# Retention and a gated feed-forward layer on one core: exponential decay tables, both first loads split over two queues, and the last 128 output rows in three parts

## The chip, the cores and the metric

The kernel runs on one core of a Trainium2 chip. The metric is the device time of one execution in microseconds (us); the time of a kernel is the median of its runs. The names of the engines are those of the profile: PE is TensorE (matmuls), PEld its weight loads, DVE is VectorE, ACT is ScalarE, POOL is GpSimd, SP is SyncE. A q behind the name (SPq, ACTq) is the engine's sequencer, which issues DMAs.

## The reference

Inputs are q, k and v of shape (8, 8, 576, 64) (batch B, heads H, sequence S, head dimension D) and three weights of a feed-forward layer, w_gate and w_val (512 x 1536) and w_out (1536 x 512), all in float32. The first stage is a retention without softmax, the second a layer with a sigmoid gate:

```
scale = 1 / sqrt(D);  gamma[h] = 1 - 2 ** (-5 - h)
scores = scale * (q @ k^T)                         # per batch and head
Dmat[h, i, j] = gamma[h] ** (i - j) if i >= j else 0
attn = (scores * Dmat) @ v                         # (B, H, S, D)
x = attn.transpose(0, 2, 1, 3).reshape(B * S, H * D)   # 4608 x 512
out = (sigmoid(x @ w_gate) * (x @ w_val)) @ w_out      # 4608 x 512, float32
```

Since gamma ** (i - j) is gamma ** i times gamma ** -j, the decay can be put on q and k ahead of the product: q is multiplied by scale * gamma ** i and k by gamma ** -j.

## The kernel before

**Stages.** The order of all instructions is written out by hand (a manual schedule); each engine and each queue runs its own in that order. The first 768 output columns of x (transposed, `xT`) come from three "pairs" of 256 tokens (`PAIRS`), the rest from steps of 128 tokens (`STEPS`), whose work is put between the matmuls of the feed-forward blocks (`BLOCKS`, of 256 to 512 tokens). PE's work from about 17 us to the end is thus a continuous row of feed-forward matmuls (`h_units`, `op_units`) with the retention's small products in between.

**First loads.** `load_pair` brings the pairs in tiles of 256 KB (`k32p`, `q32p`, `v32p`: 128 partitions, four heads, two rows of 64 numbers per partition, 512 bytes in a row). For the first two pairs the order on SP is k and q of heads 0 to 3, k and q of heads 4 to 7 of pair 0, the same of pair 1, then the four v tiles, then the weights. SP issues them one after the other; only the very first k tile goes out in two halves, from SP and from ScalarE (L130). The tiles of all loads come from a pool of 18 buffers, so a later load waits for the cast that frees its buffer.

**Decay tables.** Two pairs of small tables hold gamma ** -j for k and scale * gamma ** i for q: `ktab2`, `qtab2` for the pairs (positions step by 2 over partitions), `ktab`, `qtab` for the steps. The class `Tables` makes them: GpSimd writes the positions (`iota`), VectorE multiplies them by ln gamma for each of the eight heads (`args`, L207), ScalarE takes two sigmoids, of the argument and of its negative (`sigmoids`, L210 and L211), and VectorE makes the powers out of their quotients (`powers`, L214 to L216: one reciprocal and two products). The second tables' work is interleaved: four args, the first tables' powers, four args, the sigmoids; their powers come after the first q cast (L876). ScalarE's only tables in the kernel are thus those of the sigmoid, which the gate needs too. `lnscale` and `warm`, which the change adds, are not there.

**First products.** `cast_pair` (L288) multiplies a loaded tile by its table and writes bf16, k on GpSimd and q on VectorE; v is cast on GpSimd (L285). `turn` (`pair_t`) transposes a cast tile on PE against the identity (L328) and copies the result out on ScalarE (L338). `pair_qk` (L347) makes the scores, which VectorE masks (L352); `first_st` (L383) the state products; `tile_sv` (L401) copies the state into a block-diagonal tile `sbd`, four of which are set to zero ahead of use (two at L238, two at L878). `fill` (L188) runs matmuls on a zero tile whose results nobody reads. The order on PE is: kT, qT of heads 0 to 3, a fill, the scores, kT, a fill, qT of heads 4 to 7, a fill, and so on with pair 1.

**The end.** `op_units` multiplies the gated tokens `gvs` (12 chunks of 128) by `wo_sb`. For every 128 rows there are 12 matmuls of 512 columns into a bank of PSUM (L809), a copy on ScalarE and a store by SP (`store`, `leave`, L780). The last 128 rows (L793 to L806) go in two halves of 256 columns: 12 matmuls (L798), a copy on VectorE and a store from SP for the first half; 12 matmuls, a copy on ScalarE and a store from ScalarE's queue for the second. Three banks (`ffn_psum`) take the results of all of these in turn.

Of the kernel before, what the change touches and what calls it, by code (L numbers as in the profile page):

```python
# [9 lines left out]
FP32 = mybir.dt.float32  # L10
BF16 = mybir.dt.bfloat16
AF = mybir.ActivationFunctionType
ALU = mybir.AluOpType
# [3 lines left out]
def kernel(  # L17
# [19 lines left out]
    nc = tc.nc  # L37

    B, H, S, D = q.shape
    NT, DM = out.shape  # L40
    DFF = moe_w_gate.shape[1]
    P = 128
    M = H // 2
    NC = (S + P - 1) // P
# [3 lines left out]
    consts = ctx.enter_context(tc.tile_pool(name="consts", bufs=1))  # L48
# [5 lines left out]
    osb_pool = ctx.enter_context(tc.tile_pool(name="osb", bufs=13))  # L54
# [6 lines left out]
    ffn_psum = ctx.enter_context(tc.tile_pool(name="ffn_psum", bufs=3, space=PS))  # L61
# [5 lines left out]
    LAST = NC - 1  # L67
# [23 lines left out]
    def rows(col, n):  # L91

        out_ = []
        for c0 in sorted(rows_of):
            for r0, w in rows_of[c0]:
                lo, hi = max(c0, col), min(c0 + w, col + n)
                if lo < hi:
                    x = (lo - col, r0 + lo - c0, hi - lo)
                    if out_ and out_[-1][1] + out_[-1][2] == x[1]:
                        out_[-1] = (out_[-1][0], out_[-1][1], out_[-1][2] + x[2])  # L100
                    else:
                        out_.append(x)
        return out_


    def half(x):
        return slice(x * 64, x * 64 + 64)
# [17 lines left out]
    def load_pair(A):  # L125

        b, a2 = PAIRS[A]
        for nm, src, g in (("k", k, 0), ("q", q, 0), ("k", k, 1), ("q", q, 1), ("v", v, 0), ("v", v, 1)):
            t = ld_pool.tile([P, M, 2, D], FP32, tag="ld", name=f"{nm}32p_{A}_{g}")
            queues = (nc.sync, nc.scalar) if A == 0 and g == 0 and nm == "k" else (nc.sync,)  # L130
            n = M // len(queues)
            for i, queue in enumerate(queues):
                queue.dma_start(  # L133
                    out=t[:, i * n:(i + 1) * n].rearrange("p h r d -> p h (r d)"),
                    in_=src[b, g * M + i * n:g * M + (i + 1) * n,
                            a2 * 2 * P:(a2 + 1) * 2 * P, :].rearrange("h (p r) d -> p h (r d)", r=2))
            parts[nm, "pair", A, g] = t
            yield
# [11 lines left out]
    def load_wo(f):  # L150
        t = ld_pool.tile([P, DM], FP32, tag="ld", name=f"wo32_{f}")
        nc.sync.dma_start(out=t, in_=moe_w_out[f * P:(f + 1) * P, :])
        parts["o", f] = t

    both = [load_pair(A) for A in range(2)]
    for n_pair in (4, 2):
        for one in both:
# [5 lines left out]
    load_w(4, 4)  # L163
    load_w(8, 4)
    pair_2 = load_pair(2)
    for n_wo, n_pair in ((2, 4), (6, 2), (4, 0)):
        for _ in range(n_wo):
# [16 lines left out]
    def fill(n, parts=1):  # L184

        for i in range(n * parts):
            k = 4 // parts
            nc.tensor.matmul(idle[-1][:, 0:k, :], lhsT=blank, rhs=blank.unsqueeze(1).to_broadcast([P, k, P]),  # L188
                             start=True, stop=True)

    fill(10, 4)
    class Tables:


        def __init__(self, shape, pattern, step, put):
            def tile_of(name, dims):
                return consts.tile(dims, FP32, name=f"{name}{step}")
            self.put = put
            self.pos = tile_of("pos", [P, pattern[0][1], pattern[1][1]])
            nc.gpsimd.iota(self.pos, pattern=pattern, base=0, channel_multiplier=step,  # L200
                           allow_small_or_imprecise_dtypes=True)
            self.arg, self.q, self.k = (tile_of(name, shape) for name in ("arg", "qtab", "ktab"))
            self.both, self.inv = (tile_of(name, [P, 2] + shape[1:]) for name in ("both", "inv"))

        def args(self, heads):
            for h in heads:
                nc.vector.tensor_scalar_mul(self.put(self.arg, h), self.pos, math.log(1.0 - 2.0 ** (-5.0 - h)))  # L207

        def sigmoids(self):
            nc.scalar.activation(out=self.both[:, 0], in_=self.arg, func=AF.Sigmoid)  # L210
            nc.scalar.activation(out=self.both[:, 1], in_=self.arg, func=AF.Sigmoid, scale=-1.0)  # L211

        def powers(self):
            nc.vector.reciprocal(out=self.inv, in_=self.both)  # L214
            nc.vector.tensor_tensor(out=self.k, in0=self.both[:, 1], in1=self.inv[:, 0], op=ALU.mult)
            nc.vector.scalar_tensor_tensor(out=self.q, in0=self.both[:, 0], scalar=1.0 / math.sqrt(D),  # L216
                                           in1=self.inv[:, 1], op0=ALU.mult, op1=ALU.mult)

    tabs2 = Tables([P, 2, H, 2], [[2 * P, 2], [1, 2]], 2, lambda t, h: t[:, :, h, :])
    tabs2.args(range(H))  # L220
    tabs2.sigmoids()
    qtab2, ktab2 = tabs2.q, tabs2.k
    ident = consts.tile([P, P], BF16)
    make_identity(nc, ident)


    tabs1 = Tables([P, NC, H, 1], [[P, NC], [1, 1]], 1, lambda t, h: t[:, :, h, :])
    nc.vector.tensor_scalar_add(tabs1.pos[half(1), LAST], tabs1.pos[half(1), LAST], -64.0)
    tabs1.args(range(M))
    tabs2.powers()  # L230
    tabs1.args(range(M, H))
    tabs1.sigmoids()
    qtab, ktab = (t.rearrange("p c h o -> p c (h o)") for t in (tabs1.q, tabs1.k))


    sbd = [consts.tile([P, M, P], BF16, name=f"sbd{i}") for i in range(4)]
    for t in sbd[:2]:
        nc.vector.memset(t, 0.0)  # L238

    trip = consts.tile([P, 2, P], BF16)  # L240
# [1 line left out]
    for p0 in (0, 64):  # L242
        nc.gpsimd.affine_select(out=trip[p0:p0 + 64], in_=trip[p0:p0 + 64], compare_op=ALU.is_ge, fill=0.0,
                                base=0, pattern=[[-1, 2], [1, P]], channel_multiplier=-2)
# [12 lines left out]
    wo_sb = consts.tile([P, NFC, DM], BF16)  # L257
# [6 lines left out]
    on_pool, on_act, on_dve = nc.gpsimd.tensor_copy, nc.scalar.copy, nc.vector.tensor_copy  # L264
# [10 lines left out]
    def cast_pair(nm, A, g, eng):  # L275

        if (nm, A) not in natural:
            natural[nm, A] = osb_pool.tile([P, 2, H, D], BF16, tag="osb", name=f"{nm}p_{A}")
        if nm != "v" and A == 2:
            o = natural[nm, A].rearrange("p r (m y) d -> p y m r d", y=2)[:, g]  # L280
        else:
            o = natural[nm, A][:, :, g * M:(g + 1) * M, :].rearrange("p r h d -> p h r d")
        i = parts.pop((nm, "pair", A, g))
        if nm == "v":
            eng(out=o, in_=i)  # L285
        else:
            tab = (ktab2 if nm == "k" else qtab2)[:, PAIRS[A][1], g * M:(g + 1) * M, :].unsqueeze(3).to_broadcast([P, M, 2, D])
            eng.tensor_tensor(out=o, in0=i, in1=tab, op=ALU.mult)  # L288
# [493 lines left out]
    def store(opp, r0, eng=None):  # L782

        ob = osb_pool.tile([P, DM], FP32, tag="osb", name=f"ob_{r0}")
        (eng or on_act)(out=ob, in_=opp)  # L785
        stores.append((r0, ob))
        if len(stores) > KEEP:
            leave()

    def op_units(gvs, t0, n):  # L790
        for nb in range(n // P):
            r0 = t0 + nb * P
            if r0 == NT - P:  # L793

                for i, queue in enumerate((nc.sync, nc.scalar)):
                    opp = ffn_psum.tile([P, 256], FP32, tag="ffn", name=f"op_{t0}_{nb}_{i}")
                    for fc in range(NFC):
                        nc.tensor.matmul(opp, lhsT=gvs[fc][:, nb * P:(nb + 1) * P],  # L798
                                         rhs=wo_sb[:, fc, i * 256:(i + 1) * 256],
                                         start=(fc == 0), stop=(fc == NFC - 1))  # L800
                    ob = osb_pool.tile([P, 256], FP32, tag="osb", name=f"ob_{r0}_{i}")
                    (nc.vector.tensor_copy if i == 0 else nc.scalar.copy)(out=ob, in_=opp)
                    for p0, at_row, w in rows(r0, P):
                        queue.dma_start(out[at_row:at_row + w, i * 256:(i + 1) * 256], ob[p0:p0 + w])
                    yield 6 * 512
                return  # L806
            opp = ffn_psum.tile([P, 512], FP32, tag="ffn", name=f"op_{t0}_{nb}")
            for fc in range(NFC):
                nc.tensor.matmul(opp, lhsT=gvs[fc][:, nb * P:(nb + 1) * P], rhs=wo_sb[:, fc, :],  # L809
                                 start=(fc == 0), stop=(fc == NFC - 1))  # L810
                if fc % 4 == 3 and fc < NFC - 1:
                    yield 4 * 512
            store(opp, t0 + nb * P)
            yield 4 * 512
# [14 lines left out]
    gvs = {}  # L829
# [43 lines left out]
    turn("k", 0, 0, *TR)  # L873
    turn("q", 0, 0, *PV)
    fill(3)
    tabs1.powers()  # L876
    for t in sbd[2:]:
        nc.vector.memset(t, 0.0)  # L878
    cast_pair("q", 0, 1, nc.vector)
    pair_qk(0, 0, QK)  # L880
    turn("k", 0, 1, *TR)
# [233 lines left out]
```

## Time and profile before

| what | value |
|---|---|
| median of 3 runs (lowest to highest) | 331.42 us (330.25 to 331.87) |
| the profiled execution: time, span | 331.87 us, 330.2 us |
| mean granted TensorE clock | 1.000 |
| PE busy | 320.9 us, 97% of the span |
| PEld, DVE, ACT, POOL busy | 169.5, 149.9, 139.3, 104.8 us |
| read from HBM, written | 37.75 MB, 9.44 MB |
| narrow matmuls of the last rows (L798) | 24, 273 ns each from start to end, 0.11 us from one start to the next |
| ACT table loads (L210) | 1, 1283 ns |
| args for 4 and for 5 positions per head (L207) | 8 of 207 ns and 8 of 316 ns in the mean |
| powers: reciprocals (L214), products (L215, L216) | 553 and 634 ns; 193 and 761, 184 and 186 ns |

The span runs from the first to the last instruction of the profiled execution; its whole time is 1.7 us longer. Matmuls are pipelined, so the busy time of one (273 ns) is more than what it adds to a row of them. Slices, groups, chain and timeline of one execution belong together; another run of the same kernel differs by up to 1.6 us here.

### The profile page before, as it was taken

The page shows a single profiled execution, that of the slowest core. Times are in us where ns is not written, and L with a number is a line of the kernel's source. Part 1 is how long each engine was busy: PE and PEld are TensorE (multiplying, and loading weights), DVE is VectorE, ACT ScalarE, POOL GpSimd, SP SyncE. Part 2 cuts the span into 40 slices and gives each one's busy share as a digit, 9 for nine tenths or more (in the row PEclk, how much of TensorE's full clock was granted, in tenths as well). Part 3 has the DMA queues.
Part 4 walks back from the last instruction along what each step waited for, and adds up shares of the span by engine and source line. Part 5 has one row for each costly group of instructions (what it writes and reads, how often), then busy time and mean ns, then how long its engine had stood idle before and what let it go on. Part 6 is the DMA issues. An engine that isn't in the chain of part 4 may idle for free.

```text
span 330.2 us, 8760 instructions
## 1 busy us (share of the span) xinstructions
PE 320.9 (97%) x3618; PEld 169.5 (51%) x3618; DVE 149.9 (45%) x340; ACT 139.3 (42%) x315; POOL 104.8 (32%) x138
## 2 busy tenths in 40 slices
PE   7899999998999999999999999999999999999996
PEld 5564557845645654445444544455445544544443
DVE  8845637655624454345343543434435444404310
ACT  4664555554424344325433453335334533343321
POOL 5585545534545563108400750065003000000000
PEclk9999999999999999999999999999999999999999
DMA  7999999999999999948992699259904910010003
GB/s 205 293 358 379 336 280 214 187 144 192 183 196 190 214 199 226 215 92 154 221 222 45 131 238 229 45 108 230 208 0 92 333 59 0 33 68 34 2 32 95
DMA packets 145833, 55.14 MB, mean 167 GB/s; under 512 B 125184, under 2 KB 137728, under 8 KB 145792
## 3 DMA queue, kind: packets, MB, share of 16 engines
q1 hardware_dynamic: 145376, 54.31, 76.5%
q8 instruction: 28, 0.46, 0.6%
q10 hardware_dynamic: 416, 0.26, 0.2%
q14 instruction: 13, 0.11, 0.1%
HBM read 37.75 MB, written 9.44 MB: 143 GB/s over the span
## 4 chain that ended last, share of the span: by engine, by line
PE 91%; DMA 4%; SPq 2%; DVE 1%; ACT 1%; issue 0%; POOL 0%; ACTq 0%
PE h L742 50%; PE op L809 23%; PE op L994 3%; PE hg L846 3%; PE hv L846 3%; DMA T<-qk 2%; SPq L133 2%; PE val L553 2%; DMA v32p<-in_v_dram 2%; PE row L527 1%; PE val L569 1%; PE row L535 1%; PE op L798 1%; PE hg L920 1%; PE hv L920 1%; PE st L383 0%
## 5 line engine op out<-in xcount | busy, mean ns | idle before, releaser
L770 DVE TENSOR_TENSOR gv<-g,h 128x512 bf16<-128x512 bf16 (+1 forms) x96 | 62.9, 655 | 103.5 <-PE h L742 99.3
L742 PE MATMUL h<-xT,wv_sb 128*128 128x512 bf16 (+2 forms) x432 | 100.7, 355 | 0.0
L742 PE MATMUL h<-xT,wg_sb 128*128 128x512 bf16 (+2 forms) x432 | 100.7, 355 | 0.0
L766 ACT ACTIVATE g<-h 128x512 bf16<-128x512 f32 (+1 forms) x96 | 54.8, 571 | 95.5 <-PE h L742 91.3
L809 PE MATMUL op<-wo_sb,gv 128*128 128x512 bf16 x372 | 84.0, 379 | 0.0
L742 PEld LDWEIGHTS <-wg_sb 128*128 128x128 bf16 x432 | 42.0, 98 | 41.1
L742 PEld LDWEIGHTS <-wv_sb 128*128 128x128 bf16 x432 | 42.0, 98 | 40.3
L809 PEld LDWEIGHTS <-gv 128*128 128x128 bf16 x372 | 35.3, 98 | 41.0
L301 POOL TENSOR_TENSOR qk<-k,ktab 128x512 bf16<-128x512 f32 x30 | 31.4, 1045 | 42.7 <-DMA k<-in_k_dram 40.8
L306 POOL CAST v<-v 128x512 bf16<-128x512 f32 x29 | 17.7, 611 | 82.0 <-PE val L553 75.4
L785 ACT COPY ob<-op 128x512 f32<-128x512 f32 x33 | 19.4, 586 | 36.4 <-PE op L809 35.7
L301 POOL TENSOR_TENSOR qk<-q,qtab 128x512 bf16<-128x512 f32 x28 | 29.2, 1043 | 3.7 <-DMA q<-in_q_dram 3.0
L542 DVE TENSOR_TENSOR pt<-row,tri 128x256 bf16<-128x256 f32 x60 | 21.6, 418 | 15.6 <-PE row L535 13.9
L611 ACT CAST xT<-val 128x256 bf16<-128x256 f32 x46 | 15.0, 380 | 22.8 <-PE val L569 19.7
L654 DVE TENSOR_TENSOR s<-s,row 128x256 f32<-128x256 f32 x39 | 16.3, 417 | 1.3
L503 ACT CAST sb<-s 128x256 bf16<-128x256 f32 x44 | 15.9, 420 | 0.3 <-DVE s L654 0.2
L597 DVE COPY glance<-val 128x1 f32<-128x1 f32 x24 | 2.8, 155 | 23.4 <-PE val L569 22.7
L994 PE MATMUL op<-wo_sb,gv 128*128 128x512 bf16 x48 | 11.7, 379 | 0.0
L527 PE MATMUL row<-T 64*64 64x64 bf16 x480 | 9.6, 197 | 1.5 <-DMA T<-qk 1.5
L569 PE MATMUL val<-T,sb 64*64 64x64 bf16 x368 | 9.9, 195 | 0.3 <-DVE glance L597 0.3
L553 PEld LDWEIGHTS <-v 64*64 64x64 bf16 x480 | 6.2, 108 | 7.5 <-issue 7.5
L846 PE MATMUL hg<-xT,wg_sb 128*128 128x512 bf16 x40 | 9.2, 379 | 0.0
(108 smaller groups left out, 232.7 us busy)
## 6 DMA issues: line engine op xcount, KB each, us to landing
out_dram<-ob SPq DMA_DIRECT2D x31, 256.0 KB, 3.3
k<-in_k_dram SPq DMA_DIRECT2D x26, 256.0 KB, 4.0
q<-in_q_dram SPq DMA_DIRECT2D x26, 256.0 KB, 4.7
v<-in_v_dram SPq DMA_DIRECT2D x26, 256.0 KB, 5.3
wg<-in_moe_w_gate_dram SPq DMA_DIRECT2D x12, 256.0 KB, 5.7
wv<-in_moe_w_val_dram SPq DMA_DIRECT2D x12, 256.0 KB, 5.4
wo<-in_moe_w_out_dram SPq DMA_DIRECT2D x12, 256.0 KB, 5.3
q32p<-in_q_dram SPq DMA_DIRECT2D x6, 256.0 KB, 5.9
```

What stands on the lines that cost most here:

```text
L301: eng.tensor_tensor(out=natural_qk[s][:, i].rearrange("p m (y d) -> p y m d", y=2), in0=by_halves(loaded[s][1 - i]), in1=tab, op=ALU.mult)
L306: eng(out=natural["v", s], in_=loaded[s][2])
L503: eng(out=state[key], in_=src)
L542: nc.vector.tensor_tensor(out=probs[s][:, y], in0=row_ps[s][y][:, 0], in1=tri.unsqueeze(1).to_broadcast([P, M, 64]), op=ALU.mult)
L654: nc.vector.tensor_tensor(out=new, in0=running[b], in1=p, op=ALU.add)
L742: nc.tensor.matmul(out, lhsT=w_sb[:, kc, fc * P:(fc + 1) * P], rhs=xT[:, kc, t0 + a:t0 + e], start=(kc == 0), stop=(kc == NKC - 1))
L766: nc.scalar.activation(out=g[:, 0:n], in_=h1[:, 0:n], func=AF.Sigmoid)
L770: nc.vector.tensor_tensor(out=gvs[some[0]][:, a:e], in0=g[:, 0:n], in1=h2[:, 0:n], op=ALU.mult)
L785: (eng or on_act)(out=ob, in_=opp)
L809: nc.tensor.matmul(opp, lhsT=gvs[fc][:, nb * P:(nb + 1) * P], rhs=wo_sb[:, fc, :], start=(fc == 0), stop=(fc == NFC - 1))
L846: nc.tensor.matmul(ps, lhsT=(wg_sb if what == "g" else wv_sb)[:, kc, fc * P:(fc + 1) * P], rhs=xT[:, kc, 0:4 * P], start=(kc == 0), stop=( ...
L994: nc.tensor.matmul(opps[nb], lhsT=gvs[fc][:, nb * P:(nb + 1) * P], rhs=wo_sb[:, fc, :], start=(fc == 0), stop=(fc == NFC - 1))
```

## The change

**Loads.** The first q tile is split in halves over SP and ScalarE, as the first k tile is.

**Tables.** A function `tables` takes the place of the class. ScalarE makes both tables of a set by two exponentials: exp(-argument) for k, and exp(argument + ln scale) for q, the logarithm as a bias per partition from `lnscale`, which VectorE sets. The sigmoids, the reciprocals and the products are gone. All eight args of the second set follow one another, and its exponentials follow them at once. After them ScalarE runs one sigmoid of a single column into `warm`, which nobody reads; from there on the sigmoid's table is needed in place of the exponential's. All four `sbd` tiles are set to zero ahead of the first q cast.

**The last 128 rows.** They go in parts of 256, 128 and 128 columns: the first is copied by ScalarE and stored by SP, the second copied by VectorE and stored by SP, the third copied by ScalarE and stored from ScalarE's queue.

```diff
-            queues = (nc.sync, nc.scalar) if A == 0 and g == 0 and nm == "k" else (nc.sync,)
+            queues = (nc.sync, nc.scalar) if A == 0 and g == 0 and nm != "v" else (nc.sync,)
...
-        def sigmoids(self):
-            nc.scalar.activation(out=self.both[:, 0], in_=self.arg, func=AF.Sigmoid)
-            nc.scalar.activation(out=self.both[:, 1], in_=self.arg, func=AF.Sigmoid, scale=-1.0)
-
-        def powers(self):
-            nc.vector.reciprocal(out=self.inv, in_=self.both)
-            nc.vector.tensor_tensor(out=self.k, in0=self.both[:, 1], in1=self.inv[:, 0], op=ALU.mult)
-            nc.vector.scalar_tensor_tensor(out=self.q, in0=self.both[:, 0], scalar=1.0 / math.sqrt(D),
-                                           in1=self.inv[:, 1], op0=ALU.mult, op1=ALU.mult)
...
-    tabs1.args(range(M))
-    tabs2.powers()
-    tabs1.args(range(M, H))
-    tabs1.sigmoids()
...
+    def tables(shape, pattern, step, put, fix=None):
+
+        pos = consts.tile([P, pattern[0][1], pattern[1][1]], FP32, name=f"pos{step}")
+        nc.gpsimd.iota(pos, pattern=pattern, base=0, channel_multiplier=step,
+                       allow_small_or_imprecise_dtypes=True)
+        if fix:
+            fix(pos)
...
+        for h in range(H):
+            nc.vector.tensor_scalar_mul(put(arg, h), pos, math.log(1.0 - 2.0 ** (-5.0 - h)))
+        nc.scalar.activation(out=kt, in_=arg, func=AF.Exp, bias=0.0, scale=-1.0)
+        nc.scalar.activation(out=qt, in_=arg, func=AF.Exp, bias=lnscale, scale=1.0)
+        return qt, kt
+
+    lnscale = consts.tile([P, 1], FP32)
+    nc.vector.memset(lnscale, math.log(1.0 / math.sqrt(D)))
+    qtab2, ktab2 = tables([P, 2, H, 2], [[2 * P, 2], [1, 2]], 2, lambda t, h: t[:, :, h, :])
...
+    qtab, ktab = tables([P, NC, H, 1], [[P, NC], [1, 1]], 1, lambda t, h: t[:, :, h, :], last_chunks)
...
+    warm = consts.tile([P, 1], FP32)
+    nc.scalar.activation(out=warm, in_=lnscale, func=AF.Sigmoid)
...
-    for t in sbd[:2]:
+    for t in sbd:
         nc.vector.memset(t, 0.0)
...
-                for i, queue in enumerate((nc.sync, nc.scalar)):
-                    opp = ffn_psum.tile([P, 256], FP32, tag="ffn", name=f"op_{t0}_{nb}_{i}")
+                for i, (c0, w, queue, eng) in enumerate(((0, 256, nc.sync, on_act), (256, 128, nc.sync, on_dve),
+                                                         (384, 128, nc.scalar, on_act))):
+                    opp = ffn_psum.tile([P, w], FP32, tag="ffn", name=f"op_{t0}_{nb}_{i}")
                     for fc in range(NFC):
-                        nc.tensor.matmul(opp, lhsT=gvs[fc][:, nb * P:(nb + 1) * P],
-                                         rhs=wo_sb[:, fc, i * 256:(i + 1) * 256],
+                        nc.tensor.matmul(opp, lhsT=gvs[fc][:, nb * P:(nb + 1) * P], rhs=wo_sb[:, fc, c0:c0 + w],
                                          start=(fc == 0), stop=(fc == NFC - 1))
...
-                    (nc.vector.tensor_copy if i == 0 else nc.scalar.copy)(out=ob, in_=opp)
+                    eng(out=ob, in_=opp)
...
-    tabs1.powers()
-    for t in sbd[2:]:
-        nc.vector.memset(t, 0.0)
     cast_pair("q", 0, 1, nc.vector)
```

More of the change, by code (lines that the diff above doesn't have):

```diff
@@ L191 @@
     fill(10, 4)
[L192 to L207, printed above, removed]
-        def sigmoids(self):
-            nc.scalar.activation(out=self.both[:, 0], in_=self.arg, func=AF.Sigmoid)
-            nc.scalar.activation(out=self.both[:, 1], in_=self.arg, func=AF.Sigmoid, scale=-1.0)
-        def powers(self):
-            nc.vector.reciprocal(out=self.inv, in_=self.both)
-            nc.vector.tensor_tensor(out=self.k, in0=self.both[:, 1], in1=self.inv[:, 0], op=ALU.mult)
-            nc.vector.scalar_tensor_tensor(out=self.q, in0=self.both[:, 0], scalar=1.0 / math.sqrt(D),
-                                           in1=self.inv[:, 1], op0=ALU.mult, op1=ALU.mult)
@@ L219 @@
[L219 to L222, printed above, removed]
+    def tables(shape, pattern, step, put, fix=None):
[4 more added lines that the diff above has]
+            fix(pos)
+        arg = consts.tile(shape, FP32, name=f"arg{step}")
+        qt = consts.tile(shape, FP32, name=f"qtab{step}")
+        kt = consts.tile(shape, FP32, name=f"ktab{step}")
+        for h in range(H):
[3 more added lines that the diff above has]
+        return qt, kt
@@ L223 @@
+    lnscale = consts.tile([P, 1], FP32)
+    nc.vector.memset(lnscale, math.log(1.0 / math.sqrt(D)))
+    qtab2, ktab2 = tables([P, 2, H, 2], [[2 * P, 2], [1, 2]], 2, lambda t, h: t[:, :, h, :])
     ident = consts.tile([P, P], BF16)
     make_identity(nc, ident)
-    tabs1 = Tables([P, NC, H, 1], [[P, NC], [1, 1]], 1, lambda t, h: t[:, :, h, :])
-    nc.vector.tensor_scalar_add(tabs1.pos[half(1), LAST], tabs1.pos[half(1), LAST], -64.0)
-    tabs1.args(range(M))
-    tabs2.powers()
-    tabs1.args(range(M, H))
@@ L232, with last_chunks @@
-    tabs1.sigmoids()
-    qtab, ktab = (t.rearrange("p c h o -> p c (h o)") for t in (tabs1.q, tabs1.k))
+    def last_chunks(pos):
+        nc.vector.tensor_scalar_add(pos[half(1), LAST], pos[half(1), LAST], -64.0)
+    qtab, ktab = tables([P, NC, H, 1], [[P, NC], [1, 1]], 1, lambda t, h: t[:, :, h, :], last_chunks)
+    qtab = qtab.rearrange("p c h o -> p c (h o)")
+    ktab = ktab.rearrange("p c h o -> p c (h o)")
+    warm = consts.tile([P, 1], FP32)
+    nc.scalar.activation(out=warm, in_=lnscale, func=AF.Sigmoid)
@@ L793, in op_units @@
             if r0 == NT - P:
-                for i, queue in enumerate((nc.sync, nc.scalar)):
-                    opp = ffn_psum.tile([P, 256], FP32, tag="ffn", name=f"op_{t0}_{nb}_{i}")
+                for i, (c0, w, queue, eng) in enumerate(((0, 256, nc.sync, on_act), (256, 128, nc.sync, on_dve),
+                                                         (384, 128, nc.scalar, on_act))):
+                    opp = ffn_psum.tile([P, w], FP32, tag="ffn", name=f"op_{t0}_{nb}_{i}")
                     for fc in range(NFC):
-                        nc.tensor.matmul(opp, lhsT=gvs[fc][:, nb * P:(nb + 1) * P],
-                                         rhs=wo_sb[:, fc, i * 256:(i + 1) * 256],
+                        nc.tensor.matmul(opp, lhsT=gvs[fc][:, nb * P:(nb + 1) * P], rhs=wo_sb[:, fc, c0:c0 + w],
                                          start=(fc == 0), stop=(fc == NFC - 1))
[L801 to L805, printed above, removed]
+                    ob = osb_pool.tile([P, w], FP32, tag="osb", name=f"ob_{r0}_{i}")
+                    eng(out=ob, in_=opp)
+                    for p0, at_row, n_row in rows(r0, P):
+                        queue.dma_start(out[at_row:at_row + n_row, c0:c0 + w], ob[p0:p0 + n_row])
+                    yield 12 * w
                 return
```

## The prediction

> **What bounds the kernel now.** I read the page first, then the chain of waits, then the timeline of the first 17 us and of the last 7 us, then the groups of matmuls and activations by form, the windows by stage, and the DMA answer for the end. The page's busy times, its slices and the chain by engine and line:
>
> ```profile
> PE 320.9 (97%) x3618; PEld 169.5 (51%) x3618; DVE 149.9 (45%) x340; ACT 139.3 (42%) x315; POOL 104.8 (32%) x138
> ...
> PE   7899999998999999999999999999999999999996
> ...
> DMA  7999999999999999948992699259904910010003
> ...
> PE 91%; DMA 4%; SPq 2%; DVE 1%; ACT 1%; issue 0%; POOL 0%; ACTq 0%
> ```
>
> TensorE (PE) is the bound. Its lighter slices are the first two, the ninth (66 to 74 us) and the last, so a change at the two ends can only work on what PE waits for there. The chain of waits says what that is:
>
> ```profile
> 4.07 1.12 SPq L133
> 5.24 1.00 SPq L133
> 6.28 1.08 SPq L133
> 7.41 5.52 DMA v32p<-in_v_dram
> 12.99 0.63 POOL vp L285
> 13.66 0.49 PE st L383 x6
> ...
> 324.24 2.63 PE op L798 x24
> 326.90 0.37 ACT ob L802
> ```
>
> At the start the chain runs through SP's load issues and the landing of the second v tile into GpSimd's cast at 12.99, then into the first state product at 13.66. Neither the tables nor ScalarE's copies are on it. At the end it is the 24 narrow matmuls, one ScalarE copy, and then a store. From the timeline of the start, the rows that the tables touch:
>
> ```profile
> 1.31 1.28 ACT L210 ACT_TABLE_LOAD   x1 [1.31 <-PEq L1099]
> 2.26 0.72 DVE L207 TENSOR_SCALAR arg<-pos 128x5 f32<-128x5 f32 x4
> 3.79 1.26 DVE L207 TENSOR_SCALAR arg<-pos 128x5 f32<-128x5 f32 x4
> 3.91 1.12 POOL L288 TENSOR_TENSOR kp<-k32p,ktab 128x512 bf16<-128x512 f32 x1 [0.96 <-DVE qtab L216]
> 5.52 0.59 ACT L338 COPY kT<-kTp 128x512 bf16<-128x512 bf16 x1
> 6.39 1.04 POOL L288 TENSOR_TENSOR kp<-k32p,ktab 128x512 bf16<-128x512 f32 x1 [1.36 <-DMA k32p<-in_k_dram]
> 6.63 0.73 ACT L338 COPY qT<-qTp 128x512 bf16<-128x512 bf16 x1 [0.53 <-PE qTp L328]
> 12.42 0.73 ACT L338 COPY qT<-qTp 128x512 bf16<-128x512 bf16 x1
> ```
>
> To see: the one table load, the first cast of k that waits 0.96 us for the tables, and the second that waits 1.36 us for its load whatever the tables do. The last rows, from the timeline of the end:
>
> ```profile
> 326.10 0.54 SPq L804 DMA_DIRECT2D out_dram<-ob  x1
> 326.90 0.37 ACT L802 COPY ob<-op 128x256 f32<-128x256 f32 x1 [2.03 <-PE op L798]
> 327.30 0.36 ACTq L804 DMA_DIRECT2D out_dram<-ob  x1
> ```
>
> After the issue at 327.30 the span still runs 2.9 us, to 330.2. The whole profiled execution took 331.87 us, 1.7 us around its span, and lies 0.45 us above the median of 331.42. Sums below are made on its span and then taken from the median. The runs spread over 1.6 us, so about 0.5% is what a measurement of this kernel can tell from no change.
>
> **The end, part by part.** Before, each half has 12 matmuls of 256 columns at 2.63/24 = 0.110 us. The nearest row for 128 columns with weights of its own is the turn in the chain of waits, 8 in 0.45 us, or 0.056 each. Parts 1 and 2 together are 24 x 0.056 = 1.34 us where 12 x 0.110 = 1.32 us were: +0.02. The last matmul itself is shorter, 219 ns against 273 ns in the groups by form: -0.05. The last copy on ScalarE falls from 372 ns (L802) to 272 ns (L633, a 128x128 copy): -0.10. The last store carries 64 KB in place of 128 KB. In the DMA answer for 323 to 331 us, forty slices of 0.2 us, the last data fill two slices at 317 and 292 GB/s; half of that is -0.2 us. The new rows are 512 bytes, which no store of this trace has. The bounds are 0 (a packet of half the size takes as long) and -0.2; I take -0.2, because the first q loads also come in 512-byte rows and run at the 293 GB/s of the second slice.
>
> Part 0's copy moves from VectorE (0.42) to ScalarE (0.37), whose store copy before it ended at 324.87, so it waits for nothing. SP is still issuing earlier stores until 326.01, so part 0's issue stays near 326.10. Part 1 ends on PE near 326.25, its VectorE copy of 0.29 (L639) near 326.54, and SP is free at 326.64: its issue stands behind part 0's there and nothing is queued behind it. SP's stores land 2.3 us after issue at the median, queueing included, which would be 328.95. ScalarE's last would be at 327.17 + 1.75 - 0.2 = 328.7, where 1.75 is how long the last store took from issue to landing. SP's data would follow part 0's by 327.9, so I take ScalarE's as last. The sum for the end is -0.33, with bounds of 0 and -0.4. I write -0.3.
>
> **The start, part by part.** Loads: the first q tile goes out in halves from SP and ScalarE. SP has as many issues as before, its half takes what the whole took (0.46 each), so every later load leaves SP at the same time, and the bytes ahead of the v tiles are the same. That is 0 on the chain, whose cover is the loads themselves. What can move is a dip: in forty slices of 0.2 us from 1 to 9 us the loads fall from 300 to between 138 and 230 GB/s from 3.8 to 4.8 us, just after the second queue's half of k has landed. Its loss against 300 GB/s is about 0.4 us; I bound this edit by -0.4 and +0.4 and take 0.
>
> ScalarE: one more issue (0.48) pushes the table load from 1.31 to 1.81 and its end to 3.09. Two exponentials at the pace of L210 and L211 end by 3.5, so the first table is there at 3.35, not at 3.77, since VectorE's reciprocal and products are gone. GpSimd's first cast can start when k has landed, 0.80 + 2.8 = 3.6: 0.3 us earlier, and then it waits longer for the load at 6.39. Gain on the chain: 0.
>
> VectorE: one more memset (0.11), then eight args in a row. At the 0.18 us of the first four they end near 3.8. The second four took 1.26 us beside GpSimd's cast, so those that fall behind its start at 3.65 may be held to its end at 4.8. Four memsets at 0.27 follow, then the first q cast at 4.9 to 5.9 (5.51 before).
>
> ScalarE again: the args release two exponentials (0.45), then the second table load (1.28, the only row there is) and the warm sigmoid (0.2); queued behind it are the copies of kT and qT, and PE waits for those. kT's copy starts at 5.75 to 6.75 (5.52 before), qT's at 6.35 to 7.35 (6.63 before): between 0.3 early and 0.7 late. What hides the 0.7: VectorE's second set of powers and two memsets (0.63 + 0.76 + 0.19 + 0.55) no longer stand ahead of the second q cast, which started at 8.07 and can start when its load lands, near 7.2; that gives back about 0.2. The last ScalarE copy of qT ended at 13.15, and the first state product that the chain has waits for v until 13.66: another 0.5. So the sum of the start is 0, and what is next late is that v tile, as before. Were the cover gone, the price would be the 0.7.
>
> Against this change speaks the Trainium skill, page "ScalarE: Activation LUTs", section "What ACT_TABLE_LOAD costs": a switch of table sets costs the load of about 1283 ns and a drain of about 1380 ns. The trace agrees on the load (1283 ns) and shows no drain: the first sigmoid starts at 2.61, 0.02 us after it. By the page's estimate the copies would be late by up to 2.1 us, and the start would cost up to 1.4.
>
> **Sum.** 331.42 - 0.3 + 0 = 331.1 us, 331.6 for an execution like the profiled one. The case's own range is 330.4 to 331.9, from -0.4 and +0.4 for the loads and 0 to -0.4 for the end, rounded outward for the scatter.
>
> **Rivals.** First, slower: ScalarE becomes the bound of the start. Place: the second table load ahead of the first kT copy. I bound its price above by twice the row, 2.57 us. With the args held as well, qT's copy is 0.7 + 1.3 = 2.0 us late, and after the cover of 0.7 the first state product is 1.3 us late. It decides once the lateness passes 0.7. For it: every copy of the first stage goes through ScalarE, which runs without a pause from 10.75 to 13.15. Against it: this later row,
>
> ```profile
> 75.24 0.32 PE L527 MATMUL row<-T 64*64 64x64 bf16 x16 [1.07 <-DMA T<-qk]
> ```
>
> The windows by stage give PE 6.50 of 8.00 us from 68 to 76 us, so 1.5 us of waiting there can swallow a late start, unless the loads are late with it, because casts free their buffers. Then nothing is swallowed, and the later copies may slip on top: 331.1 + 1.3 = 332.4 at least, to about 333.7 if the whole 2.0 and some slipped loads show; I name 332.9. Second, faster: two queues keep the loads at 300 GB/s (-0.4), and half of the 1.5 us of waiting at 68 to 76 us goes with it (-0.75): 331.1 - 1.15 = 329.95. For it: that stretch waits for DMAs. Against it: the bytes are the same. Third, the end saves nothing, because SP's store of part 1 lands last at 328.95 or the small rows are slow: 331.4.
>
> **How the numbers follow.** Forecast 0.56, slower start 0.25, faster loads 0.13, no gain at the end 0.06. Slower by over 0.5% is above 333.1: about half of the first rival and, by scatter, a little of the rest, 0.17. Faster by over 0.5% is below 329.8: half of the second rival and a little of the forecast, 0.10. Within: 0.73. The range reaches to 329.7 and 333.3, so as to leave out the outer parts of both rivals.
>
> **What would show it.** Right: the chain still goes through the v32p landing near 13 us and st L383 starts within 0.3 us of 13.66; two table loads of 1.28 us; narrow matmuls at 0.056; the last copy at 0.27; from the last issue to the end of the span 2.7 us. Wrong: ScalarE's kT or qT copies releasing PE at 13 us or later, a second load followed by idle time on ScalarE, a granted clock under 1.0 in the first 17 us, other waits at 68 to 76 us, or SP's store as the last to land.

## The result, and the profile after

The changed kernel takes 328.17 us (median of 6 runs, 327.98 to 328.49), the kernel before 331.64 us beside it (6 runs, 330.25 to 332.18). The ratio is 0.990, with an interval of 0.988 to 0.992: 3.5 us less, where 0.3 us was forecast. The profiled execution took 327.98 us and has a span of 326.3 us, 3.9 less than before.

The page after has these lines in place of those shown:

```profile
PE 320.6 (98%) x3630; PEld 169.9 (52%) x3630; DVE 147.7 (45%) x335; ACT 140.8 (43%) x318; POOL 104.1 (32%) x138
...
PE   8999999999999999999999999999999999999996
...
DMA  7999999979999999909890999069704910010003
...
PE 95%; ACT 3%; DVE 1%; ACTq 0%; issue 0%
```

PE is as busy as before. What changed is the waiting: the light slice at 66 to 74 us is gone, and no DMA and no SP issue is left on the chain that ended last. The chain of waits after (start, length, what):

```profile
1.86 1.28 ACT L204
...
3.94 1.28 ACT L222
...
5.94 0.70 ACT qT L327
...
11.52 0.66 ACT qT L327
12.18 0.05 issue
12.23 0.62 PE st L372 x8
...
320.75 2.66 PE op L788 x36
```

At the start the chain now runs through the two table loads and ScalarE's copies. The state products on it start at 12.23 us, not at 13.66. Before, PE ran the first two of them at 13.21, right behind ScalarE's copy of qT, and only the other six waited for the second v tile; the timeline before has this row for the two:

```profile
13.21 0.28 PE L383 MATMUL st<-vp,kp 64*128 64x128 bf16 x2 [0.48 <-ACT qT L338]
```

In the timeline after, ScalarE's second table load with its neighbours, and the first two v casts, read:

```profile
3.15 0.23 ACT L204 ACTIVATE ktab<-arg 128x32 f32<-128x32 f32 x1
...
3.94 1.28 ACT L222 ACT_TABLE_LOAD   x1
...
5.24 0.20 ACT L222 ACTIVATE warm<-lnscale 128x1 f32<-128x1 f32 x1
5.35 0.58 ACT L327 COPY kT<-kTp 128x512 bf16<-128x512 bf16 x1
...
10.72 1.38 POOL L274 CAST vp<-v32p 128x512 bf16<-128x512 f32 x2 [0.33 <-DMA v32p<-in_v_dram]
```

Those casts began at 12.07 and 12.99 us before. The issues of the loads up to 3.4 us stand within 0.05 us of where they stood before; the data come faster. The windows by stage (length, busy time of PE, PEld, DVE, ACT and POOL, each with its instructions, granted clock, DMA share, GB/s), first of the kernel before:

```profile
8.00:14.00 6.00, 4.80 (x70) 2.63 (x67) 5.32 (x10) 3.73 (x6) 3.55 (x5) 1.00 1.16 293
68.00:76.00 8.00, 6.50 (x145) 3.46 (x144) 2.83 (x11) 3.33 (x10) 3.34 (x4) 1.00 1.36 190
```

and of the changed kernel:

```profile
8.00:14.00 6.00, 5.20 (x117) 3.52 (x115) 5.55 (x10) 4.33 (x9) 4.28 (x6) 1.00 1.14 340
68.00:76.00 8.00, 8.00 (x106) 4.48 (x105) 5.11 (x15) 4.70 (x14) 3.63 (x5) 1.00 0.70 148
```

From 8 to 14 us the loads run at 340 GB/s in place of 293, and at 68 to 76 us PE no longer waits. In the trace's record of the packets, one of 512 bytes takes 27.3 ns in the mean from 8 to 14 us, where it took 32.1 before, and one of 2048 bytes from 22 to 26 us takes 84.0 ns in place of 87.8. The end, from the timeline:

```profile
322.10 0.37 ACT L791 COPY ob<-op 128x256 f32<-128x256 f32 x1 [0.72 <-PE op L788]
322.61 1.03 SPq L793 DMA_DIRECT2D out_dram<-ob  x2
322.77 0.29 DVE L791 COPY ob<-op 128x128 f32<-128x128 f32 x1 [8.99 <-PE op L788]
323.44 0.27 ACT L791 COPY ob<-op 128x128 f32<-128x128 f32 x1 [0.97 <-PE op L788]
323.73 0.37 ACTq L793 DMA_DIRECT2D out_dram<-ob  x1
```

From the first narrow matmul's start to the end of the span it is 6.07 us before (324.08 to 330.15) and 5.68 after (320.59 to 326.27): 0.39 less. The rest had been won by then. The first matmul of the feed-forward's blocks starts at 53.15 us before and at 51.48 after, 1.7 us earlier, and most of the rest comes from 62 to 76 us. What PE waited for there before is not itself a load but a transposing DMA, which SP issues behind the loads of the step:

```profile
68.97 6.23 DMA T<-qk
```

No such DMA is on the chain after.

### The profile page after: what moved, and what is told of

Same layout as the page of the kernel before. It is cut to its first block, busy times and chain, and to the rows that moved or that the text cites. A ratio compares the mean times of both kernels' runs of the same rounds, so it can differ in the third digit from the quotient of the medians.

```text
span 326.3 us, 8784 instructions
## 1 busy us (share of the span) xinstructions
PE 320.6 (98%) x3630; PEld 169.9 (52%) x3630; DVE 147.7 (45%) x335; ACT 140.8 (43%) x318; POOL 104.1 (32%) x138
## 4 chain that ended last, share of the span: by engine, by line
PE 95%; ACT 3%; DVE 1%; ACTq 0%; issue 0%
PE h L731 51%; PE op L798 25%; PE op L980 3%; PE hg L835 3%; PE hv L835 3%; PE val L542 2%; PE row L516 1%; PE row L524 1%; PE val L558 1%; ACT qT L327 1%; PE op L788 1%; PE hg L906 1%; PE hv L906 1%; PE qkp L336 1%; PE st L372 1%; ACT kT L327 0%
## 5 line engine op out<-in xcount | busy, mean ns | idle before, releaser
L842 DVE TENSOR_TENSOR gv<-g,hv 128x512 bf16<-128x512 bf16 x10 | 6.8, 685 | 5.8 <-PE hv L835 5.8
```

## The experiments

The new theory came from the built programs' memory map, in which the starts below are read; the traces do not show addresses. The tables' extra tiles (`both` and `inv`, 1152 bytes per partition) lie ahead of the load tiles in SBUF; the change drops them and adds `lnscale` and `warm` (64 bytes with their padding). All load tiles thus move down by 1088 bytes. They are 2048 bytes apart, so they share one remainder: they started at 320 modulo 512 before and start at 256 after. Theory A: that start sets the rate of the loads. Theory B: the split of q does, by the second queue. Theory C: the tables' order on the engines is worth the time. Theory D: the runs stood under other conditions.

The kernel before was run beside each group, and its median moved between 330.77 and 331.83 us from group to group. A ratio below is to the kernel before beside it.

**Alignment alone, on the kernel before (b_at256).**

```diff
-            self.arg, self.q, self.k = (tile_of(name, shape) for name in ("arg", "qtab", "ktab"))
+            self.arg, self.q = (tile_of(name, shape) for name in ("arg", "qtab"))
+            self.k = self.arg if step == 2 else tile_of("ktab", shape)
...
     glance = consts.tile([P, NJ], FP32)
+    consts.tile([P, 16], FP32, name="pad")
```

> The kernel before, with one alteration: the first k table is written over its own arguments and 64 bytes per partition stay unused, so that the load tiles start at a multiple of 256 bytes in SBUF (256 modulo 512, as in the changed kernel) and not at 320 modulo 512. Instructions and queues are the same. Theory A (the start of the load tiles sets the loads' rate): loads from 8 to 14 us at about 345 GB/s as in the changed kernel, not 290; first state product near 12.2 us; 328.5 us. Theory B (the second queue's half of q sets it): 290 GB/s, 331.6 us. Theory C (the tables' instructions on ScalarE and VectorE): 331.6 us. Theory D (the runs stood under other conditions of the chip): whatever the kernel before shows beside it.

Measured: 329.63 us, ratio 0.993 (0.991 to 0.996). Its windows:

```profile
8.00:14.00 6.00, 5.12 (x89) 2.99 (x89) 5.91 (x10) 3.83 (x7) 5.18 (x6) 1.00 1.06 311
68.00:76.00 8.00, 7.84 (x139) 4.49 (x128) 4.50 (x14) 3.73 (x12) 3.05 (x4) 1.00 0.67 143
```

A 512-byte packet took 27.7 ns and PE's wait at 68 to 76 us fell from 1.5 to 0.2 us. About 2 us of the 3.5 come with no change to any instruction but the place of its data. It fell short of the 328.5 that theory A gave it, because the first state product still starts behind ScalarE's copy of qT:

```profile
13.24 0.62 PE L384 MATMUL st<-vp,kp 64*128 64x128 bf16 x8 [0.48 <-ACT qT L339]
```

The earlier v tiles alone thus gave only 0.3 us at this place (the eighth product ends at 13.86 us, before at 14.15). Up to the first matmul of the feed-forward's blocks it is 0.7 us (52.49 us against 53.15); the larger part came later, from 62 to 76 us.

**Alignment taken away from the changed kernel (a_pad64).**

```diff
     glance = consts.tile([P, NJ], FP32)
+    consts.tile([P, 16], FP32, name="pad")
```

> The changed kernel with 64 unused bytes per partition ahead of the load tiles, which puts their start at 320 modulo 512 as in the kernel before. Theory A: back to 290 GB/s from 8 to 14 us, 331.2 us (331.6 less the 0.4 that the end saves). Theories B and C: 345 GB/s, 328.2 us. Theory D: the same as the changed kernel, and both move with the chip.

Measured: 331.62 us, ratio 1.000 (0.997 to 1.003). The whole gain is gone:

```profile
8.00:14.00 6.00, 4.26 (x61) 2.22 (x60) 4.92 (x9) 3.76 (x6) 3.31 (x4) 1.00 1.16 291
68.00:76.00 8.00, 6.82 (x147) 3.69 (x146) 4.17 (x13) 3.60 (x10) 3.31 (x4) 1.00 1.33 186
```

The packets take 32.4 ns. With 64 unused bytes, tables, split and end together are worth nothing that can be measured; by the interval, at most 0.9 us. Theory B falls with this run, and C as the main cause. Theory D falls with the group: b_at256 was faster than the kernel before beside it, and a_pad64 was not.

**The split of q alone (b_qsplit)**: the one line of the change at L130, on the kernel before.

> The kernel before with the first q tile split over the two queues and nothing else. Theory A: 290 GB/s, 331.6 us. Theory B: 345 GB/s, 328.6 us. Theory C: 331.6 us.

Measured: 331.34 us, ratio 0.999 (0.997 to 1.001), 292 GB/s from 8 to 14 us, 32.6 ns a packet. As theory A has it.

**The end alone (b_tail)**: the change's loop over three parts, on the kernel before.

> The kernel before with the last 128 rows in parts of 256, 128 and 128 columns and nothing else. All theories: the stretch from the first narrow matmul to the end of the span falls from 5.96 to 5.6 us, and the time by 0.3 to 0.4 us, to 331.3 us; loads as before.

Measured: 331.27 us, ratio 0.999 (0.997 to 1.002), 0.25 us under the kernel before. The stretch from the first narrow matmul to the end of the span fell by 0.3 us, from 6.07 to 5.75. The median alone could not tell so little from nothing.

**Which tiles count (a_ld320, a_rest320).** The first moves the load tiles alone to 320, the second only the pools behind them.

```diff
# a_ld320: 64 bytes ahead of the load tiles as in a_pad64, and
+    ctx.enter_context(tc.tile_pool(name="pad_after", bufs=1)).tile([P, 112], FP32, name="pad_after")
     nat_pool = ctx.enter_context(tc.tile_pool(name="nat", bufs=5))
# a_rest320: nothing ahead, and
+    ctx.enter_context(tc.tile_pool(name="pad_after", bufs=1)).tile([P, 16], FP32, name="pad_after")
     nat_pool = ctx.enter_context(tc.tile_pool(name="nat", bufs=5))
```

> The changed kernel with 64 unused bytes per partition ahead of the load tiles and 448 behind them: only the load tiles move to 320 modulo 512, and the pools behind them (work tiles, transposed tiles, output tiles) go back to 256 modulo 512. Theory A1 (the start of the load tiles alone sets the rate): 32 ns for a 512-byte packet and 290 GB/s from 8 to 14 us, 331.4 us. Theory A2 (it is the start of the tiles behind them, which engines, transposes and stores use): 27 ns and 340 GB/s, 328.2 us.

> The changed kernel with 64 unused bytes per partition behind the load tiles: these stay at 256 modulo 512, and the pools behind them (work tiles, transposed tiles, output tiles) move to 320. Theory A1 (the load tiles' start alone counts): 27 ns for a 512-byte packet, 340 GB/s from 8 to 14 us, 328.2 us. Theory A2 (the pools behind count as well): between 328.6 and 331 us.

Measured: 330.96 us, ratio 0.999 (0.997 to 1.002), for the load tiles at 320, and 328.18 us, ratio 0.989 (0.984 to 0.994), for the others at 320. Their windows, first with the load tiles moved:

```profile
8.00:14.00 6.00, 4.89 (x87) 2.98 (x87) 4.78 (x8) 4.00 (x7) 3.86 (x5) 1.00 1.17 292
```

then with the rest moved:

```profile
8.00:14.00 6.00, 5.20 (x115) 3.50 (x113) 5.66 (x9) 4.32 (x9) 4.72 (x6) 1.00 1.14 339
```

It is the start of the load tiles, and not that of the pools behind them.

**How coarse the step is (a_pad128, a_pad32)**: a_pad64 with 32 and with 8 numbers in place of 16, which puts the load tiles at 384 and at 288 modulo 512.

> The changed kernel with 128 unused bytes ahead of the load tiles: they start at 384 modulo 512, a multiple of 128 but not of 256. Theory A with a step of 128 bytes: 27 ns for a 512-byte packet, 340 GB/s, 328.2 us. Theory A with a step of 256 bytes: 32 ns, 290 GB/s, 331.5 us as with 64 unused bytes.

> The changed kernel with 32 unused bytes ahead of the load tiles: they start at 288 modulo 512. If only multiples of 256 are fast: 32 ns for a 512-byte packet, 290 GB/s, 331.3 us. If the loss grows with the distance from such a multiple: something between 328.2 and 331.

Measured: 330.67 us, ratio 0.999 (0.998 to 1.000), 32.3 ns a packet at 384; 331.47 us, ratio 0.999 (0.997 to 1.001), 32.4 ns at 288. Of the four starts tried (256, 288, 320 and 384 modulo 512) only 256 was fast, and the loss did not grow with the distance from it. A start at 0 modulo 512 was not tried, so that every multiple of 256 is fast is not shown.

**What the rest of the change is worth once the loads are fast (exp_at256, b_at256_q, a_noq).** The first is the changed kernel without the split and without the three parts; the second is b_at256 with the split; the third is the changed kernel without the split.

> The changed kernel without the split of the first q tile and without the three parts at the end: only the exponential tables are left of the change, with load tiles at 256 modulo 512. The kernel before with its tiles at 256 took 329.6 us. If the tables' order on VectorE and ScalarE is what bounds the start once the loads are fast: first state product near 12.3 us in place of 13.24, 328.6 us (that is, 1.0 below, the rest of the gap to 328.2 being the end). If the split of q is what is missing: 329.6 us.

> The kernel before with its load tiles at 256 modulo 512 (329.6 us), and the first q tile split over two queues besides; tables by sigmoids, two halves at the end. If the split of q is what is missing: 328.6 us and the first state product near 12.3 us. If the tables are: 329.6 us and 13.2 us.

> The changed kernel without the split of the first q tile: load tiles at 256, exponential tables and the end in three parts stay. If the split is worth nothing: 328.2 us, 0.4 under the version without the three parts (328.6). If the second issue on ScalarE costs, because it puts the first table load off by 0.5 us: 327.8 us, faster than both kernels.

Measured: exp_at256 328.60 us (0.993, 0.991 to 0.995), b_at256_q 329.79 us (0.997, 0.995 to 0.998), run in one group; a_noq 328.51 us (0.990, 0.988 to 0.993), in the group in which a_rest320, which keeps the split, took 328.18. So with loads at the fast rate the exponential tables are worth 1.0 to 1.2 us by the medians. The 1.2 is against b_at256_q, which has the split besides; the 1.0 is against b_at256, which does not, but ran in another group, and the two ratios (0.993 and 0.993) do not separate these two versions. The split is worth between nothing (329.79 against 329.63 with the sigmoids) and 0.3 us (328.18 against 328.51 with the exponentials). In exp_at256 the first state product starts at 12.35 us, in b_at256 at 13.24, in b_at256_q at 13.85, and in a_noq at 13.28. In a_noq it is the loads that came late: its second k tile landed at 7.08 us, in exp_at256 at 6.16.

**Whether that is VectorE's queue (sig_late, sig_late2).** In b_at256 the second q cast stands behind the second tables' powers and two memsets: its load landed at 7.54 us and it started at 8.09. Both versions put b_at256's second tables behind the first pairs and all four memsets ahead of the first q cast; both end in three parts.

```diff
-    tabs1.args(range(M))
     tabs2.powers()
-    tabs1.args(range(M, H))
-    tabs1.sigmoids()
...
# sig_late
+    tabs1.args(range(H))
+    tabs1.sigmoids()
     step(h_both((2, 3)), 4)
+    tabs1.powers()
...
# sig_late2 instead
     units = h_both((4, 5, 6, 7))
+    tabs1.args(range(H))
     step(units, 4)
+    tabs1.sigmoids()
+    tabs1.powers()
```

> The kernel before with its load tiles at 256 modulo 512, the end in three parts, and VectorE's queue cleared ahead of the q casts: the second tables' arguments and sigmoids go behind the first pairs (ahead of the feed-forward's third and fourth chunk), their powers after those chunks, all four zero tiles ahead of the first q cast. Tables stay sigmoids, with one table load. If what the sigmoid version loses once the loads are fast is VectorE's queue ahead of the q casts: the second q cast starts within 0.2 us of its load's landing, first state product near 12.3 us, 328.2 us, and perhaps 0.2 below the changed kernel for the missing second table load. If it is ScalarE's table work or something else: about 329.3 us (329.6 less the end).

> As the version before it (load tiles at 256, end in three parts, sigmoid tables with VectorE's queue cleared ahead of the q casts), but the second tables' arguments stand one group of chunks later, and their sigmoids and powers behind the four gates of that group, so that no gate waits for them. That version had its first state product at 12.27 us and lost 0.48 us at 24.7 us, where a gate stood behind the sigmoids. If VectorE's queue is what the sigmoid tables cost once the loads are fast: first state product near 12.3, no gap at 24.7, 328.3 to 328.9 us. If the sigmoid version loses the time elsewhere: 329.5 us again.

Measured: 329.54 us (0.996, 0.994 to 0.998) and 329.12 us (0.994, 0.992 to 0.997). In sig_late the second q cast followed its load by 0.02 us and the first state product came at 12.27 us, as expected, but PE then lost 0.48 us at 24.7. In sig_late a gate stood behind the moved sigmoids there. Sig_late2 has a gap of the same size (0.49 us at 25.0) for another reason: PE waited for a product on VectorE, which stood behind the sum of the states; that waited for a ScalarE copy behind a cast, and the cast for its weight tile. Its profiled execution is the slowest of its ten (329.98; the fastest took 328.30), with its second k tile landing at 6.83 us where sig_late had it at 5.65. There the first state product came at 13.03 us. From b_at256 to sig_late the second q cast moved from 8.09 to 6.43 us: 0.5 us of that is the wait in VectorE's queue, and 1.1 us is its load, which landed at 7.54 us in the one and at 6.41 in the other. How much of the 1 us in the first state product is VectorE's is not separated. What makes up the 1.0 to 1.2 us between the two kinds of tables is thus not shown, and stays open. Neither version beats the changed kernel.

## Why the prediction was wrong

**The step that failed** is the term for the loads at the start, put at 0: that with the same issues and the same bytes ahead of the v tiles the landing of v cannot move, a chain "whose cover is the loads themselves". The bytes were the same; the time of a packet was not, 27.3 ns in place of 32.1. The sum followed what the edit does to the instructions and left out where it moves the tiles behind the tables. With the rate at 340 GB/s in place of 293 the second v tile landed near 11.4 us, 1.5 us earlier, against bounds of 0.4 either way for this edit. By itself the start of the tiles is worth 1.9 us (b_at256), most of it not at the v tiles but from 62 to 76 us.

**The stretch at 68 to 76 us** was at 0 in the sum and served the first rival as a place that could swallow a late start. It was the second gain: with the tiles at 256 its 1.5 us of waiting went (to 0.2 us in b_at256, to nothing in the changed kernel). The second rival had this sum in the right form (0.4 and half of 1.5), and was too small in both terms; and it laid the rate to the second queue, which alone gives nothing (ratio 0.999).

**The tables**: the sum of 0 was right for the loads as they were, since a_pad64, with tables, split and end, is not faster than the kernel before, within 0.9 us. It no longer holds once the loads are fast: the chains of the changed kernel and of b_at256 then run through ScalarE's copies, and in b_at256 through VectorE's args and memsets too. The step that sized the cover took v's landing as fixed. The bounds for ScalarE were too late as well: the eight args took 0.99 us, not 1.44 or more, and were done before GpSimd's cast began at 3.82, so nothing was held; kT's copy started at 5.35 us (5.75 to 6.75 expected), qT's at 5.90.

**The first rival** (ScalarE becomes the bound of the start, by the second table load) had the place right and the price wrong. The chain after does run through that load and ScalarE's copies, but they are not late: the load takes 1283 ns, the next activation follows at once, at 5.24 us after a load begun at 3.94, and the copy of kT starts 0.17 us earlier than before. The drain of about 1380 ns that the Trainium skill, page "ScalarE: Activation LUTs", section "What ACT_TABLE_LOAD costs", adds to each switch of sets does not show here, in either of the two loads.

**The end** was right in kind and size: 0.33 forecast, 0.39 between the two profiles, 0.3 in the profile of the end alone. The narrow matmuls, the copy of 0.27 us and the last issue stood where the sum put them; ScalarE's store was the last to land. From the last issue to the end of the span it is 2.54 us, not 2.7.

The effect on a packet agrees in kind with a rule of the Trainium skill, page "DMA: Bandwidth & Descriptors", section "How a descriptor splits into AXI transactions". It says that a transfer is cut into pieces of 256 bytes, and that the first piece of one that does not begin on a multiple of 256 starts at the multiple below it; it says so of reads. By that count, an estimate, a 512-byte row that starts at 320 modulo 512 takes three pieces in place of two. The runs show the loss on the written side, in SBUF, at 32, 64 and 128 bytes past 256 modulo 512. That the pieces are its cause is not shown.

## What to carry to other kernels

When a kernel waits for its loads, look at where the load tiles start in SBUF: here a start at 256 modulo 512 in place of 320 was worth 2 us by itself, and 64 unused bytes in front of them took the whole 3.5 us away. An edit that adds or drops a small tile moves every tile behind it, so two versions that differ in a table can differ in the rate of all loads; compare versions with the starts held equal before giving the difference to the instructions. And a cover (time hidden behind something longer) that is sized against a transfer is only as good as the rate of that transfer: work that was free behind slow loads came onto the chain when they sped up.

## What the runs showed of the hardware that was not expected

- From 8 to 14 us a 512-byte packet into SBUF takes 27 ns where the tiles start at 256 modulo 512 (the median of every such version) and 32 ns, with a wide spread (a tenth at 36 or more), at 32, 64 or 128 bytes past it. The rate needs more than that: three profiles with the tiles at 256 have 311, 314 and 270 GB/s from 8 to 14 us (b_at256, sig_late2, a_noq), with packets of 27 to 29 ns in the mean. In the first microseconds the difference does not show: from 2 to 4 us the kernel before has 27.4 ns too. Why it sets in only later is open.
- For packets of 2048 bytes the same start matters less: from 22 to 26 us the median is 84 ns in every version with the tiles at 256, 85 to 87 at 288 and 320, and 84 at 384. The means (87.8 in the kernel before, 84.0 after) tell less, since a few very slow packets raise them to 92 in one version at 256.
- The dip in the loads between 4 and 6 us is there with either start. With the load tiles on 256, the second k tile landed at 5.65 to 7.08 us in the profiles of the five versions that do not split q, and at 6.03 to 6.23 us in the three that do. Whether the split steadies it was not tried further.
- In one profile (the load tiles at 288) the granted clock fell for a stretch, and the execution, 331.83 us, lay within the spread of its kernel. The feed-forward's blocks began 2.0 us later than in the kernel before (55.11 us against 53.15), and PE then waited almost nothing from 68 to 76 us (7.95 us busy of 8.00):

```profile
14.00:20.00 6.00, 6.00 (x105) 4.62 (x98) 2.40 (x4) 2.41 (x7) 3.69 (x7) 0.52 1.13 320
```
